# The leftover tile's read-out between the last two transforms' halves, another order of attention's first and last steps, and the first weights' jobs two products later

## The chip, the cores and the metric

The kernel runs on one core of one Trainium2 chip. The metric is the device time of one launch in microseconds. TensorE (PE) multiplies matrices into the sum banks of PSUM, VectorE (DVE), ScalarE (ACT) and GpSimd (POOL) work on tiles of up to 128 partitions, and SyncE (SP) starts the transfers (DMA). Each engine works through its own queue in the order in which it was written, and waits there for the semaphores of other engines.

## The reference

Three layers follow one another, all in fp32:

```python
# attention: q, k, v are (2 batches, 8 heads, 576, 64); window 128, causal
scores = where(mask, q @ k.T / 8 - slope[h] * |i - j|, -1e9)
attn = softmax(scores) @ v
x = attn, back as (1152 tokens, 512)

# 4 experts, 512 -> 1024 -> 512, every token through every expert
p = probs / (probs.sum(-1) + 1e-9)
x = sum over e of p[:, e] * (relu(x @ w1[e]) @ w2[e])

# dense layer, 512 -> 2048 -> 512
h = x @ w_in
out = (h * cos(h)) @ w_out
```

## The kernel before

The 1152 tokens are nine tiles of 128. Tile 0, the leftover tile, holds the first 64 tokens of both batches; the other eight make two halves of four tiles. A product in fp32 is done as three products (PASSES) of a first part and a second part of each operand: ACT writes the first part (rounded), DVE or POOL subtracts it from the operand and so writes the second. A "transform" makes such parts for a pair of tiles.

*Layers.* The wide layers are cut into 12 groups of 512 hidden columns: g = 0 to 7 for the experts (w1t, w2t are the weights' parts, raw and sm what they are made from), g = 8 to 11 for the dense layer. The first layer of a group isn't four block products but seven (pair(), line 689 does one of them), on sums and differences of blocks of x (B11, T2, T1, T3, B21, B22, T4, held in xs and xz) and of the weights. Its results are put together on DVE (line 753: u1, c22, and sums in place) and end in finish(): ACT writes the first part of hpair (line 678), DVE the second (line 679). The leftover tile has its own first layer, left() (line 719), in two halves ("La", "Lb"). The second layer, layer2(), multiplies a tile of hpair by w2t (line 839) and adds it to an accumulator; for tile 0 of group 0 that is acc0 (line 858).

*Attention.* The two batches have nine units of queries, taken in the order 1, 2, 3, 4, 0, 5, 6, 7, 8, each in two groups of heads: 18 steps. A step has scores (att_scores, line 447), the softmax's maximum and exponentials (line 458 on DVE, 464 on ACT), transposes of the weights two steps later (att_transpose, line 512, LAG is 2), factors (att_factors, line 489: the transposes of the spread reciprocals, wide, which POOL copies from DVE's rec, lines 479 and 481), and the product with v a step after that (att_pv, line 549). A unit's result is normalised on DVE (line 559) and gets transformed.

*What fills it.* After the parts of step k, attention() calls fill(k, 0), fill(k, 1) and fill(k, 2). There, two idle matmuls stand in the first two steps (line 957, read by nobody), and in later steps the first weights' jobs, the leftover tile's two layers, and products of group 0 that are done ahead (early). move() issues the next stages of the transforms that are waiting (moved), and move_together() ends them: it takes the last tile's generator as far as its three subtractions, and then the last two tiles' remaining stages in turn. In the transforms sub() is line 177, and ACT's copies are line 342.

*Group 0.* When attention is done, its pools close and a pool of six sum banks takes their place; sums() hands out the banks in turn. steps(0) runs the ten products that are left of group 0 (seq says of which half, 0 or 1, each one is), and behind each of them as many weights' jobs as the list more has. A job of w1t is ACT's copy (line 200) and POOL's subtraction (line 177).

The order of the work is the order in which this code is written (manual_schedule); no scheduler moves it. The weights' jobs are generators, and next(jobs) issues one more piece of them.

Of the kernel before, what the change touches and what calls it, by code (L numbers as in the profile page):

```python
# [47 lines left out]
LAG = 2  # L48
# [3 lines left out]
def tile_kernel(ctx, tc, qT, kT, v, probs, w1, w2, w_in, w_out, out):  # L52
# [68 lines left out]
    def place(u):  # L121

        return (u - 1) // NP, (u - 1) % NP + 1
# [36 lines left out]
    def load_values(u):  # L160
        if u == 1:
            vt = qvp.tile([64, B, DM], F32, name="v0", tag="v0", bufs=1)
            nc.sync.dma_start(out=vt, in_=v[:, :64, :].rearrange("b s d -> s b d"))
            for b in range(B):
                v_t[b, 0] = vt[:, b]
        if u:
            b, i = place(u)
            s0, n = UNITS[i]
            v_t[b, i] = qvp.tile([128, DM], F32, name="vt", tag="vt", bufs=4)
            nc.sync.dma_start(out=v_t[b, i], in_=v[b, s0 : s0 + n, :])  # L170
# [239 lines left out]
            else:  # L410
                n -= 1

    def move_together():

        gens = moved[::-1]
        moved.clear()
        for _ in range(3):
            next(gens[0])
        while gens:
            gens = [g for g in gens if not next(g, True)]  # L420

# [158 lines left out]
    def load_units_to(k):  # L580
        while nloaded[0] < min(k, len(units)):
            load_unit(units[nloaded[0]])
            nloaded[0] += 1

    def attention(fill):
        n = len(steps)
        at = lambda k, what, *more: what(*steps[k], *more) if 0 <= k < n else None
        for k in range(n):
            if k % 2 == 0:

                load_units_to(k // 2 + 3)
                load_values(steps[k][0])
            at(k, att_scores)
            at(k - 1, att_sums)
            fill(k, 0)
            at(k - LAG, att_transpose)
            at(k - LAG, att_factors)
            fill(k, 1)
            at(k - LAG - 1, att_pv)
            fill(k, 2)  # L600

        at(n - 1, att_sums)
        at(n - 2, att_transpose)
        fill(n, 0)
        at(n - 1, att_transpose, ps_s, "s_ps")
        at(n - 3, att_pv)
        at(n - 1, att_factors)
        fill(n, 1)
        at(n - 2, att_pv)
        fill(n, 2)  # L610
        at(n - 1, att_pv)
        fill(n + 1, 0)
# [119 lines left out]
    def half(step, end):  # L732

        next(step)
        yield
        if end:
            whole(step)
# [98 lines left out]
    def tile_matmuls(ps, g, t, fs):  # L836
        for f in fs:
            for a, bb in PASSES:
                nc.tensor.matmul(  # L839
                    ps, hidden(a, f, t), w_t[2, g, f // 2][:, bb, f % 2, :],  # L840
                    start=(f == 0 and (a, bb) == PASSES[0]),
                    stop=(f == NFG - 1 and (a, bb) == PASSES[-1]),
                    skip_group_check=True,
                )
# [70 lines left out]
    with tc.manual_schedule():  # L915

        warm = ppool.tile([128, 4, 256], F32, name="warm", tag="p")
        nc.vector.memset(warm[:, 0], 0.0)
        nc.vector.memset(dens, 1e-9)
        for _ in range(WARM):  # L920
            nc.tensor.matmul(
                ps1.tile([128, 512], F32, name="o_ps", tag="o_ps")[:, :256],
                warm[:, 0, :128], warm[:, 0], start=True, stop=True,
            )
        load_units_to(2)
        constants()
        early = {}

        first = []

        def opening(j, kind):
            early[j] = pair(0, j, kind)
            return early[j]

        def leftover(end):
            if not first:
                first.append(left(0))
            return half(first[0], end)

        def tile_begun():  # L940
            opened[0, 0] = ps_s.tile([128, 512], F32, name="o_ps", tag="s_ps")
            tile_matmuls(opened[0, 0], 0, 0, range(NFG // 2))
            yield

        fills = {
            (12, 1): lambda: opening(0, 3), (13, 1): lambda: early[0],
            (14, 1): lambda: leftover(False), (15, 1): lambda: leftover(True),
            (16, 1): lambda: turn_rows(0), (17, 1): lambda: opening(1, 1),
            (18, 1): tile_begun, (19, 0): lambda: layer2(0, 0),
        }  # L950

        def fill(k, s):
            if s == 0 and k < 2:

                idle = ps1.tile([128, 512], F32, name="o_ps", tag="o_ps")
                for _ in range(2):
                    nc.tensor.matmul(idle[:, :128], ident, ident, start=True, stop=True)
            if (k, s) == (2, 0):
                for _ in range(RAWS):
                    loads_ahead()  # L960
            if (k, s) == (4, 0):
                nc.sync.dma_start(out=pr, in_=probs.rearrange("(t p) e -> p t e", p=128))
                first_bias()
            if (k, s) == (9, 0):
                routing()
            if s == 0 and 4 <= k < 18:
                for _ in range(2 if k in (13, 15) else 1):
                    next(jobs)
            step = fills.get((k, s), lambda: None)()
            if step:  # L970
                next(step)
            if (k, s) == (19, 0):
                move_together()
            else:
                move((0, 3, 2)[s])
            if step:
                next(step, None)
            if (k, s) == (19, 0):
                next(early[1])

        attention(fill)
    att.close()
# [8 lines left out]
    def steps(g):  # L991

        last, turn = g == NG1 + NG2 - 1, g == NG1 - 1
        moe = g < NG1
        early_kind = 1 if g in (0, NG1) else 0 if moe else 2
        ps = [early.pop(j, None) or pair(g, j, early_kind) for j in range(2)]
        if g == 0:
            for p in ps:  # L1000
                next(p)
            seq = [0, 1, 0, 1, 0, 0, 1, 0, 1, 1]
            more = [0] * 5 + [1] * 5
        elif g == NG1:
            seq = [0, 0, 0, 0, "X", 0, 1, 1, "0", 1, 1, 1]
            more = [0, 1, 1, 0, 0, 0, 1, 1, 0, 0, 0, 0]
        elif moe:
            seq = [0] * 7 + [1] * 7
            more = [0, 1, 1, 0, 0, 0, 0] + [0, 1, 1, 1, 1, 1, 1]
        else:  # L1010
            seq = [0] * 7 + ["0"] + [1] * 7
            more = [0, 1, 1, 0, 0, 0, 0, 0] + ([0] * 7 if last else [0, 1, 1, 0, 0, 0, 0])
        for j, m in zip(seq, more):
            if j == "X":
                yield turn_rows(g), 2, m, 0
            elif j == "0":
                yield layer2(g, 0), 2, m, 0
            else:
                yield ps[j], 1, m, 0
        nxt = None if last else left(g + 1)  # L1020
        ncv = {0: 2, "La": 3, 5: 3, 6: 3, 1: 3, 7: 3, "Lb": 2, 2: 2, 8: 2}
        if turn:
            order = (0, 1, "f0", 5, "f1", 2, "f5", 6, "f2", 3, "f6", 4, "f3", 7, "f4", 8, "f7")
            njobs = [2, 2, 0, 2, 0, 2]
        elif moe:
            order = (0, "La", 5, 6, 1, 7, "Lb", 2, 8, 3, "X", 4)
            njobs = [1] * 8
            if g == 0:
                order = ("La", 5, 6, 1, 7, 2, "Lb", 8, 3, "X", 4)
                njobs[0] = 2  # L1030
                ncv = {5: 1, 6: 2, 1: 3, 7: 3, 2: 3, "Lb": 2, 8: 2}
        elif last:
            order, njobs = ("a5", "a6", "a7", "a8", 5, 6, 7, 8, 1, 2, 3, 4), []
        else:
            order = ("a5", "a6", "a7", "a8", "La", 5, 6, 7, "Lb", 8, 1, 2, "X", 3, 4)
            njobs = [0, 0, 0, 0, 1, 1, 1, 1, 1, 1, 1, 1, 1, 1, 2]
        for k, o in enumerate(order):
            m = njobs.pop(0) if njobs else 0
            if isinstance(o, int):
                assert o == 0 or not any(c > 0 for c, _ in chains)  # L1040
                yield layer2(g, o), 2, m, ncv.get(o, 0)
            elif o[0] == "f":
                yield flip(int(o[1])), 0, m, 0
            elif o[0] == "a":
                yield ahead(g, int(o[1])), 2 if last else 1, m, 0
            elif o[0] == "L":
                yield half(nxt, o == "Lb"), 2, m, ncv.get(o, 0)
            else:
                yield turn_rows(g + 1), 2, m, 0
        if turn:  # L1050
            yield from last_flip(g + 1, nxt)
# [87 lines left out]
```

## Time and profile before

| | |
|---|---|
| device time, 3 runs | 657.98, 658.5, 660.17 us, median 658.5 |
| the profiled execution's own time | 657.96 us |
| its span | 656.2 us |
| TensorE | 640.1 us busy (98%), 3324 instructions |
| VectorE | 447.9 us (68%) |
| ScalarE | 324.9 us (50%) |
| GpSimd | 346.6 us (53%) |
| TensorE's mean granted clock | 0.997 |
| DMA | 60.64 MB, 92 GB/s over the span |

The span is the time from the first to the last instruction of the profiled execution; its own time holds 1.76 us round it. Engines overlap, so their busy times don't add up. A wait is idle time of an engine ahead of an instruction, put down to the engine whose semaphore came last by the profile. The granted clock is a share of TensorE's full speed. Line 839 and line 689, the two layers' products, hold 41% and 30% of the chain that ended last.

### The profile page before, as it was taken

To read this page: it belongs to the slowest core of one execution; us is meant where nothing else is said; L and a number is where in the kernel's file an instruction comes from. 1 tells how busy PE (TensorE), PEld (TensorE's weight loads), DVE (VectorE), ACT (ScalarE), POOL (GpSimd) and SP (SyncE) were. 2 spreads that over 40 slices of the span, in tenths; PEclk is the share of its full clock that TensorE was granted. 3 is DMA by queue.
4 is the path that set the end of the run, shared out by engine and by line. 5 is a ranking of instruction groups with operands and counts; after the bars stand their busy time and mean duration, and the time that the engine had idled before them with its cause. 6 is when DMAs were issued, how large, how long until landed. Compare 5 with 4: busy or idle time off the path is not lost.

```text
span 656.2 us, 9149 instructions
## 1 busy us (share of the span) xinstructions
PE 640.1 (98%) x3324; PEld 524.3 (80%) x3324; DVE 447.9 (68%) x778; ACT 324.9 (50%) x688; POOL 346.6 (53%) x330
## 2 busy tenths in 40 slices
PE   8999879999999999999999999999999999999988
PEld 6777667888888888888888888888878878878866
DVE  6686857969969868879779542556874564664652
ACT  6797615444443453454344331355883573673650
POOL 1677508456355364374274290393469379279340
PEclk9999989999999999999999999999999999999999
DMA  9443211606525616516334121020101102101003
GB/s 251 136 129 98 56 42 47 227 33 208 177 63 178 183 58 209 176 36 212 124 123 152 46 65 32 33 96 1 33 1 65 64 1 65 64 1 64 17 7 122
DMA packets 39421, 60.64 MB, mean 92 GB/s; under 512 B 4688, under 2 KB 21840, under 8 KB 39376
## 3 DMA queue, kind: packets, MB, share of 16 engines
q1 hardware_dynamic: 38288, 59.67, 28.5%
q8 instruction: 26, 0.43, 0.3%
q10 hardware_dynamic: 1088, 0.39, 0.2%
q14 instruction: 19, 0.16, 0.1%
HBM read 49.30 MB, written 10.75 MB: 92 GB/s over the span
## 4 chain that ended last, share of the span: by engine, by line
PE 82%; ACT 9%; DVE 5%; issue 2%; DMA 1%; POOL 1%; ACTq 0%; POOLq 0%; DVEq 0%
PE o_ps L839 41%; PE o_ps L689 30%; PE o_ps L719 4%; PE s_ps L447 2%; PE x_ps L549 2%; ACT p L464 1%; ACT u L642 1%; ACT r L643 1%; ACT u L650 1%; PE t_ps L512 1%; ACT hpair L662 1%; DVE c L753 1%; DMA k<-kT 1%; PE l_ps L745 1%; DVE p L458 1%
## 5 line engine op out<-in xcount | busy, mean ns | idle before, releaser
L839 PE MATMUL o_ps<-w2t,hpair 128*128 128x512 f32 x1140 | 270.2, 392 | 3.0 <-POOL hpair L177 2.5
L839 PEld LDWEIGHTS o_ps<-w2t,hpair 128*128 128x128 f32 x1140 | 210.8, 188 | 48.5 <-POOL hpair L177 4.7
L689 PE MATMUL o_ps<-xs,w1t 128*128 128x512 f32 x720 | 171.0, 393 | 4.6 <-ACT hpair L678 4.2
L689 PEld LDWEIGHTS o_ps<-xs,w1t 128*128 128x128 f32 x720 | 135.7, 189 | 33.6 <-ACT hpair L678 4.6
L177 POOL TENSOR_TENSOR w1t<-raw,w1t 128x512 fp32r<-128x512 f32 x48 | 64.5, 1358 | 91.1 <-ACT w1t L200 90.8
L177 POOL TENSOR_TENSOR w2t<-raw,w2t 128x512 fp32r<-128x512 f32 x48 | 64.0, 1355 | 64.0 <-ACT w2t L200 63.7
L177 POOL TENSOR_TENSOR w1t<-sm,w1t 128x512 fp32r<-128x512 f32 x48 | 64.0, 1343 | 40.2 <-ACT w1t L200 39.8
L689 PE MATMUL o_ps<-xz,w1t 128*128 128x512 f32 x288 | 71.0, 392 | 2.0 <-DVE c L753 2.0
L177 POOL TENSOR_TENSOR hpair<-u,hpair 128x512 fp32r<-128x512 f32 x32 | 41.6, 1312 | 45.9 <-ACT hpair L662 45.9
L689 PEld LDWEIGHTS o_ps<-xz,w1t 128*128 128x128 f32 x288 | 53.5, 188 | 15.2 <-DVE c L753 4.1
L299 ACT ACTIVATE cr<-cr 128x512 f32<-128x512 f32 x32 | 21.8, 681 | 79.1 <-DVE cv L293 79.1
L860 DVE SCALAR_TENSOR_TENSOR accpair<-o_ps,pr,accpair 128x512 f32<-128x512 f32 x56 | 41.3, 746 | 27.9 <-PE o_ps L839 27.9
L679 DVE SCALAR_TENSOR_TENSOR hpair<-o_ps,hpair 128x512 fp32r<-128x512 f32 x47 | 32.4, 689 | 23.3 <-ACT hpair L678 23.3
L678 ACT ACTIVATE hpair<-o_ps 128x512 fp32r<-128x512 f32 x47 | 28.1, 599 | 36.6 <-DVE o_ps L753 36.5
L200 ACT ACTIVATE w1t<-sm 128x512 fp32r<-128x512 f32 x44 | 27.3, 623 | 28.9 <-POOL sm L177 28.9
L464 ACT ACTIVATE p<-p,nmax 128x256 f32<-128x256 f32 (+2 forms) x72 | 33.6, 468 | 14.4 <-DVE nmax L458 14.3
L646 DVE SCALAR_TENSOR_TENSOR u<-r,u 128x512 f32<-128x512 f32 x36 | 30.7, 853 | 14.3 <-ACT r L643 14.2
L719 PEld LDWEIGHTS o_ps<-w1t,x 128*128 128x128 f32 x288 | 37.6, 191 | 1.7
L719 PE MATMUL o_ps<-w1t,x 128*128 128x256 f32 x288 | 38.5, 283 | 0.0
L866 DVE TENSOR_TENSOR accpair<-o_ps,accpair 128x512 f32<-128x512 f32 x23 | 15.9, 691 | 32.4 <-PE o_ps L839 32.4
L678 ACT ACTIVATE hpair<-c 128x512 fp32r<-128x512 f32 x17 | 10.7, 632 | 51.5 <-DVE c L753 50.8
L839 PE MATMUL o_ps<-w2t,h 128*128 128x512 f32 x144 | 35.4, 392 | 0.0
(131 smaller groups left out, 895.1 us busy)
## 6 DMA issues: line engine op xcount, KB each, us to landing
raw<-w SPq DMA_DIRECT2D x32, 512.0 KB, 3.7
cr<-w_in SPq DMA_DIRECT2D x16, 512.0 KB, 4.3
cr<-w_out SPq DMA_DIRECT2D x16, 512.0 KB, 3.8
wi<-cv SPq DMA_DIRECT2D x16, 256.0 KB, 3.4
wo<-cv SPq DMA_DIRECT2D x16, 256.0 KB, 2.2
raw<-wi SPq DMA_DIRECT2D x8, 512.0 KB, 3.4
raw<-wo SPq DMA_DIRECT2D x8, 512.0 KB, 3.6
qt<-qT SPq DMA_DIRECT2D x8, 256.0 KB, 4.1
```

The source lines that it names most:

```text
L177: eng.tensor_tensor(out=out, in0=a, in1=b, op=ALU.subtract)
L200: nc.scalar.activation(out=out, in_=src, func=AF.Copy)
L299: nc.scalar.activation(out=fl(hw), in_=fl(hw), func=AF.Abs)
L464: nc.scalar.activation(out=p[:, k, :wid], in_=p[:, k, :wid], func=AF.Exp, scale=-1.0, bias=nmax[:, k : k + 1], accum_out=den[:, k, 0:1],)
L646: nc.vector.scalar_tensor_tensor(out=u, in0=r, scalar=MAGIC, in1=u, op0=ALU.subtract, op1=ALU.subtract)
L678: nc.scalar.activation(out=hi, in_=src, func=AF.Relu)
L679: nc.vector.scalar_tensor_tensor(out=lo, in0=src, scalar=0.0, in1=hi.bitcast(F32), op0=ALU.max, op1=ALU.subtract)
L689: nc.tensor.matmul(ps, w(a, k, m), operand_of_x(bb, b)[:, m], start=(start and m == 0 and (a, bb) == PASSES[0]), stop=(stop and m == 1 and ...
L719: nc.tensor.matmul(ps[:, j * 256 : (j + 1) * 256], x0[:, bb, d, :], w_t[1, g, j][:, a, 0, d * 256 : (d + 1) * 256], start=(d == 0 and (a, ...
L839: nc.tensor.matmul(ps, hidden(a, f, t), w_t[2, g, f // 2][:, bb, f % 2, :], start=(f == 0 and (a, bb) == PASSES[0]), stop=(f == NFG - 1 an ...
L860: nc.vector.scalar_tensor_tensor(out=o, in0=ps, scalar=s, in1=o, op0=ALU.mult, op1=ALU.add)
L866: nc.vector.tensor_tensor(out=o, in0=ps, in1=o, op=ALU.add)
```

## The change

Five edits:

- attention(): in steps 0 to 3 the transposes of step k - 2 come ahead of the scores of step k; before, they came behind them.
- fill(): the two idle matmuls stand in step 0 alone.
- fill(): at (17, 2) move(2) is not called.
- fill() and move_together(): at (19, 0) the leftover tile's read-out (acc0) comes behind the last tile's three subtractions, ahead of the other stages of the last two transforms; before, it came behind all of them.
- steps(0): the five pieces of the weights' jobs, one each behind the products 6 to 10 before, come two behind the 8th, one behind the 9th and two behind the 10th.

```diff
-    def move_together():
+    def move_together(step):
 
         gens = moved[::-1]
         moved.clear()
         for _ in range(3):
             next(gens[0])
+        next(step, None)
         while gens:
             gens = [g for g in gens if not next(g, True)]
...
+            if k < 4:
+                at(k - LAG, att_transpose)
             at(k, att_scores)
             at(k - 1, att_sums)
             fill(k, 0)
-            at(k - LAG, att_transpose)
+            if k >= 4:
+                at(k - LAG, att_transpose)
             at(k - LAG, att_factors)
             fill(k, 1)
             at(k - LAG - 1, att_pv)
...
-            if s == 0 and k < 2:
+            if s == 0 and k < 1:
...
             if (k, s) == (19, 0):
-                move_together()
-            else:
+                move_together(step)
+                next(early[1])
+            elif (k, s) != (17, 2):
                 move((0, 3, 2)[s])
             if step:
                 next(step, None)
-            if (k, s) == (19, 0):
-                next(early[1])
...
             seq = [0, 1, 0, 1, 0, 0, 1, 0, 1, 1]
-            more = [0] * 5 + [1] * 5
+            more = [0] * 7 + [2, 1, 2]
```

The lines behind the first edit have other numbers in the new kernel, by 1 to 4 in what is shown here (447 is 448, 678 is 682, 858 is 862).

On VectorE, where the last tile's transform begins (x21_136 is the last tile, x20_135 the one before it, the names in xs, xk and xz its operands), before:

```order
L177 TENSOR_TENSOR x21_136<-x21_136 128x256
L177 TENSOR_TENSOR xs_132<-tx_1212,xs_132 128x2x128
L177 TENSOR_TENSOR xk_134<-xk_134,tx_1213 128x2x128
L177 TENSOR_TENSOR xs_132<-tx_1244,xs_132 128x2x128
L177 TENSOR_TENSOR xz_1020<-x20_135,xz_1020 128x2x128
L177 TENSOR_TENSOR xk_134<-xk_134,tx_1245 128x2x128
L177 TENSOR_TENSOR xz_1020<-xk_134,xz_1020 128x2x128
L177 TENSOR_TENSOR xz_1020<-x21_136,xz_1020 128x2x128
L177 TENSOR_TENSOR xz_1020<-xk_134,xz_1020 128x2x128
L858 TENSOR_SCALAR acc0_141<-o_ps_1205,pr_138 128x512
L679 SCALAR_TENSOR_TENSOR hpair_1299<-c11_869,hpair_1299 128x512
```

And now, in the same place:

```order
L177 TENSOR_TENSOR x21_136<-x21_136 128x256
L862 TENSOR_SCALAR acc0_141<-o_ps_1202,pr_138 128x512
L177 TENSOR_TENSOR xs_132<-tx_1209,xs_132 128x2x128
L177 TENSOR_TENSOR xk_134<-xk_134,tx_1210 128x2x128
L177 TENSOR_TENSOR xs_132<-tx_1241,xs_132 128x2x128
L177 TENSOR_TENSOR xz_1017<-x20_135,xz_1017 128x2x128
L177 TENSOR_TENSOR xk_134<-xk_134,tx_1242 128x2x128
L177 TENSOR_TENSOR xz_1017<-xk_134,xz_1017 128x2x128
L177 TENSOR_TENSOR xz_1017<-x21_136,xz_1017 128x2x128
L177 TENSOR_TENSOR xz_1017<-xk_134,xz_1017 128x2x128
L683 SCALAR_TENSOR_TENSOR hpair_1296<-c11_866,hpair_1296 128x512
```

The read-out acc0 has moved up past eight operations; nothing else on VectorE has changed places there.

On TensorE, at the start, from the second scores on (s_ps the scores, o_ps<-ident the idle pair, t_ps the transposes), before:

```order
L447 MATMUL s_ps<-k_156,qt 128x192 x4
L957 MATMUL o_ps<-ident 128x128 x2
L447 MATMUL s_ps<-k_156,qt 128x256 x4
L512 MATMUL t_ps<-ident,p 64x128 x2
L512 MATMUL t_ps<-ident,p 128x128 x2
L512 MATMUL t_ps<-ident,p 64x128 x2
L512 MATMUL t_ps<-ident,p 128x128 x2
L447 MATMUL s_ps<-k_156,qt 128x256 x4
```

And now:

```order
L448 MATMUL s_ps<-k_156,qt 128x192 x4
L513 MATMUL t_ps<-ident,p 64x128 x2
L513 MATMUL t_ps<-ident,p 128x128 x2
L513 MATMUL t_ps<-ident,p 64x128 x2
L513 MATMUL t_ps<-ident,p 128x128 x2
L448 MATMUL s_ps<-k_156,qt 128x256 x4
L513 MATMUL t_ps<-ident,p 64x128 x2
L513 MATMUL t_ps<-ident,p 128x128 x2
```

The idle pair is gone and the transposes of the first step stand ahead of the third scores, those of the second step ahead of the fourth. (The trace counts two instructions for each matmul here.)

## Rows read from the trace of the kernel before

**Rows 1.** Waits of TensorE up to 200 us (engine, line, releaser: total, times, longest).

```profile
PE o_ps L689 <- ACT hpair L678: 4.2, 1, 4.2
...
PE o_ps L689 <- DVE c L753: 1.2, 1, 1.2
PE r_ps L489 <- POOL wide L481: 0.8, 1, 0.8
```

**Rows 2.** Windows (length, busy us and instructions of each engine, granted clock, DMA share, GB/s).

```profile
86.00:88.00 2.00, 2.00 (x6) 1.54 (x6) 1.04 (x2) 0.20 (x1) 0.00 (x0) 0.50 0.04 8
100.00:102.00 2.00, 0.96 (x4) 0.83 (x5) 1.30 (x3) 0.81 (x2) 2.00 (x3) 1.00 0.00 0
9.43:19.00 9.57, 9.39 (x78) 6.42 (x79) 6.79 (x37) 8.36 (x34) 0.61 (x1) 1.00 1.04 302
```

**Rows 3.** Timeline of the handover (start, duration, engine, line, operation, [idle before <-releaser]).

```profile
79.97 1.53 PE L689 MATMUL o_ps<-xs,w1t 128*128 128x512 f32 x6
...
80.55 0.42 DVE L177 TENSOR_TENSOR xs<-tx,xs 128x256 fp32r<-128x256 f32 x1
...
80.83 0.75 POOL L177 TENSOR_TENSOR xs<-tx,xs 128x256 fp32r<-128x256 f32 x1 [2.64 <-ACT xs L342]
80.89 0.97 DVE L177 TENSOR_TENSOR xk<-xk,tx 128x256 f32<-128x256 f32 x1
...
82.64 0.94 DVE L177 TENSOR_TENSOR xz<-x,xz 128x256 fp32r<-128x256 f32 x1
...
84.51 0.41 DVE L177 TENSOR_TENSOR xz<-xk,xz 128x256 fp32r<-128x256 f32 x1
84.85 0.74 DVE L858 TENSOR_SCALAR acc<-o_ps,pr 128x512 f32<-128x512 f32 x1
85.08 0.63 ACT L678 ACTIVATE hpair<-c 128x512 fp32r<-128x512 f32 x1 [0.71 <-DVE xz L177]
```

**Rows 4.** Timeline ahead of the handover.

```profile
72.70 1.09 PE L549 MATMUL x_ps<-pt,vt 128*64 128x128 f32 x16
...
72.99 0.41 DVE L177 TENSOR_TENSOR xk<-xk,tx 128x256 f32<-128x256 f32 x1
...
74.60 0.66 PE L489 MATMUL r_ps<-ident,wide 128*128 128x128 f32 x4 [0.80 <-POOL wide L481]
```

**Rows 5.** Timeline of group 0's products.

```profile
85.73 8.69 PE L689 MATMUL o_ps<-xs,w1t 128*128 128x512 f32 x30 [4.24 <-ACT hpair L678]
85.75 0.69 DVE L679 SCALAR_TENSOR_TENSOR hpair<-c,hpair 128x512 fp32r<-128x512 f32 x1 [0.16 <-ACT hpair L678]
86.36 0.68 DVE L679 SCALAR_TENSOR_TENSOR hpair<-o_ps,hpair 128x512 fp32r<-128x512 f32 x1
...
94.26 1.52 PE L689 MATMUL o_ps<-xz,w1t 128*128 128x512 f32 x6
...
95.62 1.52 PE L689 MATMUL o_ps<-xs,w1t 128*128 128x512 f32 x6
...
98.54 0.63 ACT L200 ACTIVATE w1t<-raw 128x512 fp32r<-128x512 f32 x1 [2.72 <-PE o_ps L689]
...
99.25 2.51 POOL L177 TENSOR_TENSOR w1t<-raw,w1t 128x512 fp32r<-128x512 f32 x2 [15.95 <-ACT w1t L200]
...
101.03 1.66 PE L689 MATMUL o_ps<-xz,w1t 128*128 128x512 f32 x6 [1.17 <-DVE c L753]
```

**Rows 6.** Timeline of TensorE behind them.

```profile
103.96 14.46 PE L839 MATMUL o_ps<-w2t,hpair 128*128 128x512 f32 x60
```

**Rows 7.** Chain of the start (start, duration, what).

```profile
8.79 0.64 PE o_ps L957 x4
9.43 1.46 PE s_ps L447 x8
...
16.19 1.06 PE s_ps L447 x8
```

**Rows 8.** Timeline of ACT at the start.

```profile
17.81 0.51 ACT L464 ACTIVATE p<-p,nmax 128x256 f32<-128x256 f32 x1 [1.21 <-DVE nmax L458]
```

## The prediction

> **What bounds the kernel now.** I went from the table to the waits of TensorE, from there to the stretch round each wait, and last to the chain of the start. TensorE is busy 98% of the span, so only what shortens its own chain can pay. Three of its waits lie near what the change moves [rows 1]: one of 4.2 us ahead of a product of layer 1, one of 1.2 us a little later, and one of 0.8 us at the transposes of the softmax factors. The stretch after the long wait costs again: for the two microseconds behind it the granted clock was 0.50, the lower of TensorE's two levels (1.2 GHz), while the stretch round the second wait shows 1.00, the upper (2.4 GHz) [rows 2].
>
> Which work ends the long wait? The trace names ACT's first pass over hpair (line 678). The program says otherwise. The product's sums take one of the banks that the attention's pools gave back, and DVE's read-out of the leftover tile (line 858, acc0) still holds it; the order shows that the matmul waits for DVE and ACT, and there ACT's word is an operand of the last tile (T2's first part). Times agree: the read-out ends at 84.85 + 0.74 = 85.59, and the product starts at 85.73, while ACT's pass runs on until 85.71 without anything in the product that reads it [rows 3, 5]. The read-out stands behind eight operations of line 177 on DVE, the first at 80.55, the last ending at 84.92 [rows 3]. Those eight are what TensorE really waits for.
>
> **Part 1, the read-out ahead of the eight.** In the changed order acc0 stands where the first of the eight stood. On the clock of before it begins at 80.55 and lasts 0.74. Another part shifts this stretch, so that comes first.
>
> **Part 2, no move at step (17, 2).** The transposes at 74.60 wait 0.80 for POOL's wide, which waits for DVE's rec, which stands behind two moved operations on DVE (the second from 72.99 to 73.40) and one on POOL [rows 4]. Without that move these come later, after rec and wide, so the transposes follow the products that start at 72.70 and last 1.09: at 73.79. That is 0.81 us sooner, and all of the next stretch with it. What isn't moved there is left to the later moves, ahead of the last tile's own. If DVE and POOL find no time for it there, the handover doesn't come sooner, and the gain is 0 instead of 0.81.
>
> **The handover with both.** acc0 runs at 79.74 to 80.48. POOL's second part of T2 (80.83 + 0.75 [rows 3]) ends at 80.77, and the early product that starts at 79.97 [rows 3] now starts at 79.16 and is through at 80.52. So the first new product starts at about 80.7, a wait of 0.1 to 0.2. With no long wait the clock stays up: the five products of T2, T1 and T3 took 94.26 - 85.73 = 8.53 us, 1.71 each, against 1.36 for one at the full clock (94.26 to 95.62) [rows 5]. Five at 1.36 end at 87.5. One wait is new in the program: the third product's second matmul waits for DVE's second part of T1, the third of the eight, with all later products behind it. Three of the eight, two of them slow, end at about 82.7, and that product is not due before 83.4, so the wait costs nothing; it would cost if the eight were 0.3 slower each.
>
> Now DVE is late, not for acc0 but for the sums. The eight operations take 4.30 us as before (80.55 to 84.85), from 80.48 to 84.78. ACT's pass follows 0.23 later, DVE's two over hpair 0.90 after the eight (85.75 against 84.85, so at 85.68), 0.61 apart, then four sums at that pitch [rows 3, 5]; the third of these (c22 of the first half) ends at about 88.8. The sixth product reads it and so waits some 1.3 us. From there products follow at 1.36: the tenth starts at 94.2, where before it started at 101.03 after its 1.17 us wait [rows 5].
>
> **Part 3, the first weights' jobs two products later.** Before, ACT's two copies of w1t (98.54, waiting 2.72 us for TensorE to let go of the old weights) stand ahead of the pass that DVE needs for c22 of the second half, and that is the 1.17 us wait [rows 5]. Now they stand behind: c22 is ready at about 94.05, and the tenth product waits for nothing. What is late next are the copies themselves: ACT reaches them at 94.7, is done at 95.9, and POOL's two subtractions (2.51 us [rows 5], from 95.3) end at 97.85. The leftover tile's layer 1 (line 719) would like to start at 95.6 and is held at its second half until then; it ends at about 98.4. Part 3 thus trades a wait of 1.17 for one of about 1.3, and I cost it at -0.1. Bounds: +1.2 if the copies find a gap and that layer doesn't wait, -1.3 if POOL's 2.51 stand open whole.
>
> Line 839 starts at 98.4 instead of 103.96 [rows 6]: 5.6 us for parts 1 to 3. Behind that the order is as before and all engines shift together.
>
> **Part 4, the start.** The second pair of idle matmuls goes (0.64 in the chain, as four records) and the transposes of the first step come ahead of the third scores. Scores and transposes are the same work in another order. The pair and both scores are pieces of the chain on TensorE itself [rows 7], so the pair's time comes free: 0.64. The third scores took 1.46, the fifth, of the same shape, 1.06 [rows 7]: 0.40 of waiting in there may go too, but the transposes of the second step then wait about 0.3 for the exponentials and the copies on ACT, which is near full in this stretch. I set these against each other. Does ACT pass the gain on? It waits 1.21 us at 17.81 for DVE's maxima of the fifth scores [rows 8], so it has room for 0.64. Bounds: -0.5 (all of it and a copy's 0.5 lost to waits) to +1.0 (0.64 + 0.40).
>
> **Sum.** 5.6 + 0.64 = 6.3 us (6.0 to 6.9) from the profiled execution's 657.96 (span 656.2) gives 651.7. The median of the runs shown is 658.5, which is 0.5 above the profiled one, and the lowest 657.98; I count from 658.3, between the two: 652.0.
>
> A rule of the Trainium skill on one term: the eight operations of 128x256 take 0.41 us alone (84.51), and 0.97 where POOL works at the same time (80.89, POOL's from 80.83 on) [rows 3]. The Trainium skill ("GPSIMD Engine Reference", Specifications) says that POOL shares its SBUF interfaces with VectorE and contends with operations that have two SBUF inputs. The trace agrees, with 0.97 against 0.41. By that rule acc0, which reads one tensor from PSUM, would not be slowed where it now stands, and the eight, which begin 0.74 later against POOL, would have one slow operation less: the sum would be about 6.8 and the time 651.5. I keep 4.30 for the eight, since the operations of the trace were shifted against POOL only by that one place.
>
> **Rivals.**
> *DVE becomes the bound.* Eight operations at the slow length of the trace (three from 80.89 to 82.64, so 0.88 apart [rows 3]) take 7.0 us instead of 4.30: the sixth product then waits 2.7 longer, 4.0 in all, and a wait of that size is what the clock fell after (the 4.24 of [rows 1, 2]); five products at 1.71 would lose another 1.7. Gain 6.3 - 2.7 = 3.6, or 1.9 with the clock: about 654.7, up to 656.4. For it: three of the eight are slow today. Against: the last of the eight takes 0.41 again [rows 3], and POOL gets no more work than before.
>
> *The trace is right and ACT's pass over hpair holds the product.* Then acc0's place does nothing. The pass begins when the eight are done, at 85.0, and the product at 85.6; the five at half the clock take 8.53 as before, so the sixth starts at 94.1 and, with the steps of the forecast behind it (98.4 - 88.8 = 9.6), line 839 at 103.7, against 103.96: with part 4 a gain of 0.9, 657.4. Against it: the program's semaphores name DVE and the operand.
>
> *Slower: the clock falls at the start.* The idle pair may be what keeps TensorE at its upper level. From 9.43 to 19.00 TensorE is busy 9.39 us at a granted clock of 1.00 [rows 2]; at 0.50 that work takes 9.4 us more, so it would be 9.4 - 6.3 = 3.1 us slower than before: 661.4. It decides from the point where more than 6.3 us of the work run at half the clock; behind the 4.24 us wait the low clock lasted for five products. Against it: in the pair's place come transposes, which are work, and a wait of 1.17 (101.03) left the clock at 1.00 [rows 2]. The Trainium skill ("TensorE: Matmul & The Clock Gate", What's actually happening) has the throttled state as the default and activity as what releases it; the 0.50 behind the 4.24 us wait agrees. By that rule the gap which the pair filled would have to become idle time for the clock to fall.
>
> *Better.* The 0.40 in the third scores is gained, the eight run quicker and the copies find a gap: 6.3 + 0.4 + 0.5 + 0.6, about 650.5.
>
> **Chances.** Forecast 0.62 (its own range 650.7 to 653.6: the bounds of part 4, and half a microsecond either way on the handover). Better 0.09. DVE bound 0.19. ACT's pass 0.05. Slower 0.05. The range that leaves out no more than two in ten: 650.0 to 655.8, which takes in the better case and most of the DVE case. A measurement of this kernel tells 0.3%, some 2 us, from no change: faster lies below 656.5, slower above 660.5. Faster: 0.62 + 0.09 + 0.19 = 0.90; same: 0.05 and one part in a hundred of the slower case, 0.06; slower: 0.04.
>
> **What the profile after would show.** Right: acc0 ending some 5 us sooner than 85.59, and the first product with a wait under 0.5; a wait of 1 to 1.5 before the sixth product on DVE's c; none at the tenth; one of about 1.3 in line 719 on POOL's w1t; a granted clock over 0.9 in the ten products; no wait at the transposes of line 489; the fifth scores at about 15.5 instead of 16.19 [rows 7]. Wrong: the first product still held until ACT's hpair; the eight at 0.9 each and a wait of 3 or more before the sixth product; a clock of 0.50 anywhere before 18 us; or, against the whole sum, a new DMA wait of TensorE behind line 839, since all weights are now wanted 6 us sooner.

## The result and the profile after

The changed kernel takes 650.66 us (median of 4 runs, 650.58 to 652.13) against 658.24 us (4 runs, 657.93 to 660.17): a ratio of 0.9881, 95% interval 0.9862 to 0.9900. The forecast was 652.0 with a range of 650.0 to 655.8. The profiled execution after has a span of 648.8 us against 656.2, a difference of 7.4. Two single executions of variants below, of 905.86 us and (the profiled one of its kernel) 1057.82 us, at mean granted clocks of 0.655 and 0.558, are left out of their medians.

TensorE's waits up to 200 us (engine, line, releaser: total, times, longest); the three lines of [rows 1] have become these:

```profile
PE o_ps L693 <- DVE c L757: 0.8, 1, 0.8
PE o_ps L723 <- POOL w1t L177: 0.6, 2, 0.3
```

The long wait is gone, and so is the one for wide. The clock did not fall (length, busy time of PE, of PEld, which is TensorE's weight loads, of DVE, ACT, POOL, granted clock, DMA share, GB/s):

```profile
84.00:86.00 2.00, 2.00 (x11) 1.65 (x10) 1.41 (x3) 1.04 (x2) 0.00 (x0) 1.00 0.00 0
86.00:88.00 2.00, 1.16 (x6) 0.69 (x5) 2.00 (x4) 0.00 (x0) 0.00 (x0) 1.00 0.00 0
```

Here is the handover in the timeline, from the factors' transposes to layer 2 (start, duration, engine, line, operation, [idle before <-releaser]):

```profile
71.85 1.09 PE L550 MATMUL x_ps<-pt,vt 128*64 128x128 f32 x16
...
72.87 0.65 PE L490 MATMUL r_ps<-ident,wide 128*128 128x128 f32 x4
...
78.25 8.73 PE L693 MATMUL o_ps<-xs,w1t 128*128 128x512 f32 x36
...
79.02 0.74 DVE L862 TENSOR_SCALAR acc<-o_ps,pr 128x512 f32<-128x512 f32 x1
...
79.30 0.74 POOL L177 TENSOR_TENSOR xs<-tx,xs 128x256 fp32r<-128x256 f32 x1 [1.27 <-ACT xs L342]
...
79.68 0.63 DVE L177 TENSOR_TENSOR xs<-tx,xs 128x256 fp32r<-128x256 f32 x1
...
79.88 6.67 PEld L693 LDWEIGHTS o_ps<-xs,w1t 128*128 128x128 f32 x30 [0.51 <-ACT xs L342]
...
79.99 1.81 POOL L177 TENSOR_TENSOR xs<-x,xs 128x256 fp32r<-128x256 f32 x2
...
80.24 0.96 DVE L177 TENSOR_TENSOR xk<-xk,tx 128x256 f32<-128x256 f32 x1
...
81.12 0.96 DVE L177 TENSOR_TENSOR xs<-tx,xs 128x256 fp32r<-128x256 f32 x1
...
83.35 0.41 DVE L177 TENSOR_TENSOR xz<-xk,xz 128x256 fp32r<-128x256 f32 x1
83.92 0.63 ACT L682 ACTIVATE hpair<-c 128x512 fp32r<-128x512 f32 x1 [0.71 <-DVE xz L177]
...
87.82 1.63 PE L693 MATMUL o_ps<-xz,w1t 128*128 128x512 f32 x6 [0.84 <-DVE c L757]
...
93.39 1.14 ACT L200 ACTIVATE w1t<-raw 128x512 fp32r<-128x512 f32 x2
...
94.08 2.54 POOL L177 TENSOR_TENSOR w1t<-raw,w1t 128x512 fp32r<-128x512 f32 x2 [12.28 <-ACT w1t L200]
...
95.42 0.98 PE L723 MATMUL o_ps<-w1t,x 128*128 128x256 f32 x6 [0.29 <-POOL w1t L177]
...
96.67 0.75 PE L723 MATMUL o_ps<-w1t,x 128*128 128x256 f32 x4 [0.27 <-POOL w1t L177]
...
97.26 13.76 PE L843 MATMUL o_ps<-w2t,hpair 128*128 128x512 f32 x60
```

The row at 78.25 holds six products, the early one and the five of T2, T1 and T3; no wait of TensorE is listed in it, but its weight loads show one of 0.51. The read-out ends at 79.76 instead of 85.59 [rows 3]; the new products begin at 79.9, four microseconds before ACT starts the pass over hpair (83.92) that the trace of before had named as the releaser. Their first weight load starts at 79.88, 0.12 behind the end of the read-out. In before it was 0.11 behind it:

```profile
85.70 8.30 PEld L689 LDWEIGHTS o_ps<-xs,w1t 128*128 128x128 f32 x30 [4.63 <-ACT hpair L678]
```

The eight operations take 79.68 to 83.76, 4.08 us. Layer 2 starts at 97.26 instead of 103.96 [rows 6].

The leftover tile's second half of layer 1, ten tile products later, starts at 110.86 against 118.26, which is 7.40 us sooner, more than the 6.70 at the start of layer 2. From there to the end the distance stays at 7.4. So 0.70 us were gained inside ten tile products that the forecast took as unchanged. In before no wait of TensorE shows there; the weight loads (PEld) show it:

```profile
105.62 0.30 PEld L839 LDWEIGHTS o_ps<-w2t,hpair 128*128 128x128 f32 x2 [0.54 <-ACT hpair L678]
...
106.35 11.65 PEld L839 LDWEIGHTS o_ps<-w2t,hpair 128*128 128x128 f32 x52 [0.43 <-DVE hpair L679]
```

The last passes over hpair came late for layer 2; in the changed kernel its 60 weight loads are one row without a wait. The ends of matmuls are modelled, so a short stop inside a row of 60 looks like busy time; two starts on either side of the row tell more than its busy time.

### The profile page after: what moved, and what is told of

The parts are those of the page before. It is cut to its first block, busy times and chain, and to the rows that moved or that the text cites. A ratio compares the mean times of both kernels' runs of the same rounds, so it can differ in the third digit from the quotient of the medians.

```text
span 648.8 us, 9141 instructions
## 1 busy us (share of the span) xinstructions
PE 637.5 (98%) x3320; PEld 522.6 (81%) x3320; DVE 448.1 (69%) x778; ACT 325.4 (50%) x688; POOL 347.7 (54%) x330
## 4 chain that ended last, share of the span: by engine, by line
PE 80%; ACT 9%; DVE 6%; issue 2%; POOL 1%; DMA 1%; POOLq 0%; ACTq 0%
PE o_ps L843 41%; PE o_ps L693 29%; PE o_ps L723 4%; ACT u L646 1%; ACT p L465 1%; ACT r L647 1%; ACT u L654 1%; PE x_ps L550 1%; PE s_ps L448 1%; ACT hpair L666 1%; DVE c L757 1%; PE t_ps L513 1%; DVE p L459 1%; DMA k<-kT 1%; PE l_ps L749 1%
## 5 line engine op out<-in xcount | busy, mean ns | idle before, releaser
L289 DVE TENSOR_SCALAR cv<-cr 128x512 int32<-128x512 int32 x32 | 33.7, 1052 | 2.6 <-DMA wo<-cv 2.6
```

The costliest lines, as they stand in the source:

```text
L289: nc.vector.tensor_scalar(out=o, in0=hw, scalar1=3, scalar2=0x3FFFFFF8, op0=ALU.logical_shift_left, op1=ALU.bitwise_and,)
```

## The experiments

The times scatter by a microsecond in places that no edit touches: ahead of another early product, at 67 to 70 us, TensorE waits for DVE's h, for 0.2 us in eight of the traces and for 1.2 in five (the read-out alone, the read-out halfway, no idle pair, and the last two kernels of the table). So each experiment is read by stretches of its own trace as well: *start*, from the second to the fifth scores; *handover*, from the early product to the second half of the leftover tile's layer 1 (118.26 and 110.86 above). These are differences of start times in the timelines, in us, each from one execution.

| kernel | median, us | start | handover |
|---|---|---|---|
| before | 658.24 | 8.26 | 38.29 |
| changed | 650.66 | 7.58 | 32.61 |
| acc0 behind the eight again | 656.8 | 7.59 | 38.33 |
| acc0 behind four of the eight | 655.57 | 7.59 | 35.94 |
| before, acc0 early alone | 653.8 | 8.34 | 33.51 |
| move(2) at (17, 2) again | 651.4 | 7.58 | 32.44 |
| jobs as before | 651.87 | 7.58 | 33.71 |
| old start, both idle pairs | 651.43 | not read | not read |
| new order, idle pair back | 653.28 | 8.10 | 32.62 |
| old order, no idle pair | 651.84 | 8.25 | 32.61 |
| no idle pair in step 0 either | 653.36 | 9.10 | 32.61 |
| first results finished late | 650.03 | 9.16 | 31.68 |
| the same, jobs one product sooner | 650.0 | 7.58 | 31.31 |
| the same, four idle matmuls | 650.62 | 7.58 | 31.30 |

**The read-out undone.** In move_together() the read-out goes back behind the loop:

```diff
-        next(step, None)
         while gens:
             gens = [g for g in gens if not next(g, True)]
...
                 move_together(step)
+                next(step, None)
                 next(early[1])
```

> The changed kernel with the read-out acc0 behind the eight transform operations again, the other edits kept. If DVE's read-out holds the bank of the first new product: acc0 ends at about 83.8 + 0.7 = 84.5, the product waits some 4.5 us, the clock falls behind it and the five products take 8.5 instead of 7.0; the 0.84 us wait of the sixth goes. About 5 us slower than the changed kernel, 655.5. If ACT's first pass over hpair (which stands where it stood) holds the product: the product starts where it starts in the changed kernel, no difference, 650.7.

Measured: 656.8 us, eleven runs from 655.12 to 657.85. TensorE's row in the timeline, and the clock behind the wait:

```profile
83.98 9.64 PE L692 MATMUL o_ps<-xs,w1t 128*128 128x512 f32 x30 [4.40 <-ACT hpair L681]
```

```profile
84.00:86.00 2.00, 2.00 (x5) 1.63 (x6) 1.28 (x2) 0.44 (x1) 0.00 (x0) 0.50 0.00 0
```

The wait (4.40), its wrong releaser and the clock of 0.50 all come back with the place of one DVE instruction; ACT's pass keeps its place in the order. The rival that ACT holds the product falls. The handover costs 5.7 us more in the profiled execution (657.82), where the row of the five products, a part of it at the low clock, took 9.64 us, against 8.69 in before [rows 5]. The fastest runs (655.1 to 655.5) lost 4.6. The profiled execution lost a further 1.6 us near the end of the kernel, of which the last section tells; that the other runs above 656 lost it there too is not shown.

**The read-out halfway.** The loop counts its rounds and calls next(step) after three of them, which is behind four of the eight operations.

> The changed kernel with the read-out acc0 behind four of the eight transform operations instead of none. If the bank that acc0 reads holds the first new product: four operations (0.63, 0.96, 0.96 and 0.41 in the changed kernel) take about 2.7 us, acc0 ends near 82.4 and the product starts there, a wait of about 2.5 us; the sixth product, which waited 0.84 for DVE, starts at 89.2 instead of 87.8, so 1.4 us slower, 652.1; up to 653.8 if the clock falls behind a wait of this length too. If ACT's first pass over hpair held it: no difference, 650.7.

Measured: 655.57 us.

```profile
83.19 0.74 DVE L865 TENSOR_SCALAR acc<-o_ps,pr 128x512 f32<-128x512 f32 x1
...
84.08 8.61 PE L696 MATMUL o_ps<-xs,w1t 128*128 128x512 f32 x30 [3.05 <-DVE acc L865]
```

The product follows the read-out wherever that stands, and now the trace itself names it: acc0 ended at 83.93, at a moment when ACT's pass had not begun (85.43). The granted clock of 84 to 86 us was 0.50 again, so a wait of 3.05 us brought the fall too. In the handover this place costs 3.3 us (35.94 against 32.61), a little above the upper end of what was expected (3.1). This profiled execution, 655.09, is 4.5 above the changed kernel's 650.58; of the 1.2 us between, about one is the wait for DVE's h, 1.2 us here and 0.2 there, ahead of the handover.

**The read-out alone.** Only the call of next(step) in move_together(), in the kernel before.

> The kernel before with the earlier read-out acc0 alone. If the edits' worths add up: the reverse of what undoing it in the changed kernel cost (4.6 us), so 4.6 faster than the kernel before, 653.7; no wait ahead of the first new product, 0.8 at the sixth, 1.17 still at the tenth. If it only pays together with the later weights' jobs: 3.4 or less, 654.9 and up.

Measured: 653.8 us, beside 658.49 for the kernel before, run together with it: 4.7 us, and 4.78 in the handover. It needs none of the other edits.

**The move undone.**

```diff
-            elif (k, s) != (17, 2):
+            else:
```

> The changed kernel with move(2) at (17, 2) called again. If the transposes' wait for wide delays all that follows: a wait of 0.8 at line 490 and 0.8 us slower, 651.5. If DVE's chain from the last tile's normalising sets the handover and the moved work is only done at another time: 0 to 0.3 slower, 650.9.

Measured: 651.4 us, 0.74 slower. The transposes of line 490 wait 0.81 for wide again, and the handover behind them is 0.17 shorter than in the changed kernel (32.44): nearly the whole wait counts.

**The jobs undone.**

```diff
-            more = [0] * 7 + [2, 1, 2]
+            more = [0] * 5 + [1] * 5
```

> The changed kernel with the weights' jobs one each behind products 6 to 10 again. As the forecast costed it: a wait of about 1.2 at the tenth product comes, the 0.6 at line 723 goes, some 0.1 to 0.6 slower, 651.1. If the jobs on ACT also make the last passes over hpair late, as the trace of before lets suspect (14.30 us for ten tile products of layer 2 against 13.60 after): another 0.7, in all 1.3 slower, 652.0.

Measured: 651.87 us, 1.21 slower; 1.10 in the handover.

```profile
87.95 1.63 PE L693 MATMUL o_ps<-xz,w1t 128*128 128x512 f32 x6 [0.84 <-DVE c L757]
...
94.85 1.67 PE L693 MATMUL o_ps<-xz,w1t 128*128 128x512 f32 x6 [1.17 <-DVE c L757]
96.36 1.60 PE L723 MATMUL o_ps<-w1t,x 128*128 128x256 f32 x12
97.80 14.46 PE L843 MATMUL o_ps<-w2t,hpair 128*128 128x512 f32 x60
112.10 1.59 PE L723 MATMUL o_ps<-w1t,x 128*128 128x256 f32 x12
```

The wait of 1.17 is back to the hundredth, the waits of line 723 are gone, and the ten tile products take 14.30 us (97.80 to 112.10) as in before, against 13.60. So the 0.70 belongs to the jobs: ACT's two copies, put between its passes over hpair, made all later passes late. The other 0.4 lies ahead of layer 2: from the sixth product to layer 2 it is 9.85 us here (87.95 to 97.80) and 9.44 in the changed kernel (87.82 to 97.26).

**The start undone, whole and in halves.** First the old order and both idle pairs; then only "k < 2" for the idle pair; then only the order (att_transpose behind fill(k, 0) for all steps).

> The changed kernel with the old order of the first steps and both idle pairs. If the idle pair lies on TensorE's chain and the order is worth nothing: 0.64 slower, 651.3. If the order gives the 0.4 in the third scores too: 1.0 slower, 651.7. If ACT doesn't pass the gain on: no difference, 650.7. The fifth scores start at 16.0 to 16.2 instead of 15.34.

> The changed kernel with the idle pair of step 1 back and the new order of the first steps. If the pair lies on TensorE's chain: 0.6 slower, 651.3. If TensorE would wait there anyway for ACT's exponentials of the first step: no difference, 650.7.

> The changed kernel with the old order of the first steps and without the idle pair of step 1. If the order only moves waits about (as the forecast set them against each other): 0 to 0.2 slower, 650.8. If the order lets ACT and DVE start the copies of the first transposes sooner and so gains by itself: 0.4 or more slower, 651.1. A granted clock under 1 in the first 20 us would show that the pair was needed in the old order.

Measured: 651.43 us (its trace isn't read), 653.28 us and 651.84 us. The second one's times scatter from 651.33 to 653.79, so the start is better read in the traces. The pair alone, taken out of before's order, gives 0.01 us (8.26 to 8.25), the order alone 0.16 (8.26 to 8.10), both 0.68 (7.58). Two traces with the old start differ by 0.08 (8.26 and 8.34), so the 0.16 is small beside the scatter; the 0.68 isn't. In the old order without the pair, TensorE waits instead:

```profile
9.99 1.13 PE L448 MATMUL s_ps<-k,qt 64*128 64x256 f32 x6 [0.58 <-DVE nmax L459]
```

The third scores need what DVE's maxima let go. The idle pair stood in that wait, and only work that doesn't need it, the first transposes, turns it into a gain.

**No idle pair at all.** "k < 0" for "k < 1".

> The changed kernel without the idle pair of step 0 as well. If only a pair that lies on TensorE's chain costs: this one runs while TensorE waits for the second units' keys (until 7.69), no difference, 650.7. If the idle pairs keep the clock up: a granted clock near 0.5 in some of the first 20 us and 3 us slower or more, 653.7.

Measured: 653.36 us, 2.7 slower. The timeline of TensorE and the stretch behind:

```profile
8.36 1.65 PE L448 MATMUL s_ps<-k,qt 64*128 64x192 f32 x8 [2.58 <-DMA k<-kT]
```

```profile
8.00:12.00 4.00, 3.64 (x18) 2.85 (x20) 1.86 (x10) 1.66 (x8) 0.00 (x0) 0.57 0.75 156
```

This is the slower rival's mechanism, one step earlier than I had put it: with nothing between the first and second scores the wait for keys is one piece of 2.58 us and the clock falls behind it. In this trace the start stretch is 1.52 us longer than the changed kernel's (9.10 against 7.58), and its second scores start 0.67 later (8.36 against 7.69); how the median's 2.7 divides isn't shown. The pair that the change removed had no such gap beside it; the one that it left has.

**Finishing the first results late.** In pair(), for group 0, finish(g, c11, f, 1) comes behind add(c22, pc, u1).

> The changed kernel with the two first results of group 0 (ACT's and DVE's passes into hpair, 0.6 us each on DVE) finished behind the first sum of c22 of their half instead of ahead of all sums. If DVE's queue ahead of the sixth product (eight operations, two passes, four sums) is what it waits for: c22 comes 1.2 us sooner, the 0.84 us wait is gone and later steps come 0.4 to 0.8 sooner, 650.0. If the later exchange between ACT and DVE (sum, first part, second part, next sum) is the bound instead: the wait comes back at the tenth product or in layer 2, no difference, 650.7. If ACT's first pass over hpair held the first product, that would now wait: 3 us slower.

**And the jobs one product sooner**, more = [0] * 6 + [2, 0, 1, 2].

> As the kernel before it, with the first two pieces of the weights' jobs one product sooner (behind the 7th, ahead of ACT's pass over c22 of the second half). If line 723's wait of 0.56 us is ACT's late copy alone: ACT starts it 1.3 us sooner, the wait goes, 649.5. If the pass that then comes 0.35 us later holds layer 2: a wait of 0.3 to 0.5 at line 843 instead, 650.0.

**And four idle matmuls** in step 0.

> The kernel with the late finish and the sooner jobs, and with four idle matmuls in step 0 instead of two. If the second units' keys come so late in some executions that the clock falls (as with none in step 0, where it cost 2.7 us): the longer filling holds the clock up there, and the spread goes; median 649.4 to 649.8. If the keys come on time: the two more lie on TensorE's chain, up to 0.6 slower, 650.3.

Measured: 650.03 us (649.6 to 652.6), 650.0 us (649.21 to 650.74) and 650.62 us (649.08 to 651.0). The sixth product no longer waits in any of the three, so DVE's queue ahead of it was its bound; the handover is 0.93, 1.30 and 1.31 us shorter than in the changed kernel. In the second, line 723 runs as one row (its weight loads wait 0.33 for POOL) and layer 2 pays 0.5 us back (14.12 us for the ten tile products instead of 13.60), as the pass over hpair that came later holds it:

```profile
98.77 3.27 PEld L846 LDWEIGHTS o_ps<-w2t,hpair 128*128 128x128 f32 x15 [0.43 <-DVE hpair L683]
```

Ratios to the kernel before are 0.9880 [0.9859, 0.9901], 0.9871 [0.9857, 0.9886] and 0.9877 [0.9857, 0.9896], against 0.9881 for the changed kernel: the gain of 1.3 us is shown in the traces, not in the times. Whether four idle matmuls take away the spread is not settled; two of five runs were at 649.1 and three at 650.6 to 651.0, and the profiled one, 650.62, had a granted clock of 1.00 and the 1.2 us wait for DVE's h. The first of the three shows the case that it was meant for: the second units' keys came late in its profiled execution (652.6), and the clock fell behind that wait, so its start took 9.16:

```profile
9.11 1.44 PE L448 MATMUL s_ps<-k,qt 64*128 64x192 f32 x8 [2.15 <-DMA k<-kT]
```

```profile
10.00:12.00 2.00, 2.00 (x12) 1.43 (x9) 1.49 (x10) 1.09 (x5) 0.00 (x0) 0.50 0.38 100
```

## Why the prediction was right

It was right in sign, place and the main mechanism, and 1.3 us short in size. In the traces, the 7.40 us at 110.86 stand against 5.56 + 0.64 forecast: about 0.7 of the difference lies in layer 2, 0.2 in the start (0.17 of it keys that came sooner), and 0.3 in the handover ahead of layer 2. The time lies just outside the forecast's own range (650.7 to 653.6) and close to the rival *Better* (650.5), but not by that rival's parts: the start gave 0.68 and not 1.04, the eight gave 0.3 of 0.5, the copies found no gap, and no case had the 0.70 of layer 2. That it came out so near is in part luck. Point by point:

- *The releaser.* Read as DVE against the trace's word, and shown by moving one instruction to three places. The part was worth 4.7 us alone.
- *No move at (17, 2).* Forecast 0.81, measured 0.74.
- *First product and clock.* The clock stayed up. A start at 80.7 in the time of before, less 0.64 for the start, is 80.1; it began at 79.9. Six products 1.36 apart, the last one 1.53 long, are 8.33 us, and the row is 8.73, so some 0.4 us of waiting lie in it, where I had 0.1 to 0.2. What it waits for was wrong too: I had POOL's second part of T2 as the last to come, but that ends at 80.04 (79.30 + 0.74), behind the start. It is still the read-out, as the first weight load follows its end by 0.11 or 0.12 us in all thirteen traces read, this one among them. An earlier place still for the read-out wasn't tried.
- *The sixth product.* Forecast a wait of 1.3, measured 0.84. The eight took 4.08 from the first start to the last end, and 4.37 by the same measure before (80.55 to 84.92 [rows 3]); the 4.30 of the forecast ran to the start of acc0. The rule of the Trainium skill ("GPSIMD Engine Reference", Specifications), that POOL contends with VectorE's operations that have two SBUF inputs, had the direction. The trace agrees: acc0, reading one tensor from PSUM, took 0.74 with POOL at work beside it (79.30), as it had alone. But of the eight, two operations remained at 0.96 and one at 0.63 (79.68 to 81.12), so they gained 0.3 us and not 0.5.
- *The jobs.* The step that was mis-sized: "Part 3 thus trades a wait of 1.17 for one of about 1.3, and I cost it at -0.1". It measured a gain of 1.2 (1.10 in the handover). The wait that it buys is listed as only 0.56 (0.29 and 0.27), but the starts tell 1.1: line 723 to layer 2 takes 2.52 us (94.74 to 97.26), and 1.44 with the jobs as before (96.36 to 97.80). So that price was near the 1.3. The trade itself came out at +0.4 and not at -0.1, as without the copies ahead of them the products ran 1.5 us sooner to the end of the tenth, more than the listed 1.17. The rest, 0.70, I had missed whole: I took layer 2 as unchanged, where ACT's later passes over hpair had held it. The trace of before had shown it, in PEld and in the distance between two rows, not in PE's waits.
- *The start.* 0.64 forecast, 0.68 measured in the traces, but for another reason than "the pair's time comes free". By itself it is worth nothing; the order gave it its worth. The two terms that I set against each other weren't independent.
- *The rivals.* DVE did not become the bound. ACT's pass is refuted. The slower rival exists, at the pair that the change kept: 2.7 us without it, the clock's part of it not divided off.

## What to carry to other kernels

When a wait has several semaphores, don't believe the named engine before its end time and its operand fit; move the instruction that you suspect and see whether the wait moves with it. Time that a filler takes isn't free for the taking: ask what the engine would wait for in its place. Here the filler's removal paid only together with a reorder (0.68 us, against 0.01). Look for short stops in the distance between starts and in the weight loads, not only in the list of waits: the list here had 0.56 where the starts had 1.1, and nothing where they had 0.70.

## What the runs showed of the hardware

The same wait can cost the clock in one execution and not in another. In the last group TensorE waits 0.25 to 0.28 and then 1.32 to 1.34 us in every trace read here. Here are TensorE's rows of before, and of the changed kernel with its read-out behind the eight, and the clock of the latter:

```profile
636.65 13.45 PE L839 MATMUL o_ps<-w2t,hpair 128*128 128x512 f32 x58 [1.33 <-POOL hpair L177]
```

```profile
634.85 15.06 PE L842 MATMUL o_ps<-w2t,hpair 128*128 128x512 f32 x58 [1.34 <-POOL hpair L177]
```

```profile
636.00:638.00 2.00, 2.00 (x6) 1.54 (x6) 0.69 (x1) 0.00 (x0) 0.03 (x1) 0.50 0.02 7
```

The 58 matmuls took 1.6 us longer in the second, and likewise 15.04 and 15.03 in two other traces of the variants (the idle pair back, no idle pair). No edit stands there. So the waits of 2.15, 2.58, 3.05 and 4.40 us were each followed by a fall, this one of 1.33 sometimes, and waits of 0.84, 1.17 and 1.37 (for the keys, in the kernel with the jobs undone) by none. What decides in the case of 1.33 stays open. It cost 1.6 us in the three traces of thirteen that have it, more than any edit but the read-out is worth in the traces. How much of the scatter of the other executions it makes isn't shown, since each kernel has one trace.
